# Selective attention followed by a SwiGLU block: attention output transposed on TensorE, bias rows copied on chip, q/k of the first head blocks on TensorE, loads re-ordered

**Chip, cores, metric.** One core of one Trainium2 chip. Times are device microseconds. Every run comes with a state, fast or slow, by its clock and its time.

## The reference, cut to what matters

```python
# q, k, v: (8 batches, 8 heads, 576, 64) f32;  s: (8, 8, 576)
scores = q @ k.T / 8 ; bias = -(cum[i] - cum[j]) with cum = cumsum(max(s, 0))
attn   = softmax(causal(scores + min(bias, 0))) @ v        # 64 heads
x      = attn, heads side by side                           # (4608 tokens, 512)
out    = (silu(x @ w_gate) * (x @ w_val)) @ w_out           # d_ff = 1536
```

The feed-forward part needs x with its 512 features on the partitions, so the attention output has to be transposed. A batch has 576 tokens, a feed-forward tile 512: tile t needs batches t-1 and t. There are nine tiles.

## The kernel before

One program order is written by hand: the heads of later batches are a generator of small items, and `pump` lays them between the matmuls of a tile. A head block is four heads. The parts that matter, with cuts marked `...`:

```python
raw bufs=2, otp bufs=2, wst bufs=2, xtp bufs=2      # SBUF buffers: raw q/k, output, raw weights, x

nc.scalar.dma_start(AUG, hl)                        # bias rows (high and low half, and negated) to DRAM
def aug(hb, eng):                                   # and from there into the k/q tiles: 4 loads a block
    ... eng.dma_start(T[...], AUG[hb * HB : ...])

def x_write(b): ...                                 # attention output of a batch to DRAM
def x_load(tt):                                     # and back, transposed by the DMA
    xts[tt] = xtp.tile([128, 4, TT], BF16, ...)
    nc.sync.dma_start_transpose(xts[tt], xdr[tt * TT : (tt + 1) * TT, :])

def side(hb, step):                                 # work for later blocks, laid beside head `step`
    ...
    if step == 0: aug(hb + 1, nc.sync); load_qk(hb + 2); cast k of hb + 1 (GpSimd)
    if step == 1: cast q of hb + 1; scratch(hb + 1)        # bf16 q/k to DRAM
    if step == 2: transposes(hb + 1)                       # and back, transposed by the DMA
    if step == 3: split(hb + 1, "k", ...); split(hb + 1, "q", ...)   # VectorE

def ffn_items(tt):
    for ft in range(12):
        pg = WG.T x (4 matmuls);  th = tanh (ScalarE);  pp = (th + 1) * pg (VectorE)
        pv = WV.T x (4 matmuls);  ht = pp * pv (VectorE)
    for ts_ in range(4):
        py = ht.T WO (12 matmuls);  copy (ScalarE);  store
```

Each engine works its own list in the order of the program, as the traces below show it (a mask on GpSimd comes only after eight copies, 4.10 us, that stand before it), and so does the queue of the SP engine, which issues nearly all loads.

Names in the profile lines: PE is TensorE, DVE VectorE, ACT ScalarE, POOL GpSimd, and a `q` behind a name is the engine's issuing of DMAs. `sc` are the scores, `pt` their exponentials (masked by GpSimd), `av` attention times V, `ot` its normalised value, `xps` the transposed `ot` in PSUM, the memory that TensorE writes, and `xt` the tile of x that `pg` and `pv` read; `xdr`, `augd`, `ks` and `qs` lie in DRAM, `pk` and `pq` are what comes back from the last two; `kq` holds k, q and the bias rows of a block, and `HL` all bias rows on chip; `wld` is a weight as loaded, `wg`, `wv` and `wo` are weights cast to bf16.

The softmax here doesn't subtract the row's maximum and nothing guards it: scores larger than these inputs give would overflow.

## Time and profile before

| | before |
|---|---|
| time | 490.84 us, median of 3 (487.07 to 491.25) |
| span of the profiled run | 486.5 us |
| busy share: TensorE / VectorE / ScalarE / GpSimd | 78 / 50 / 41 / 33 % |
| first `pg` matmul of the nine tiles | 75.4, 147.6, 196.3, 244.0, 292.0, 339.3, 382.1, 420.2, 451.3 us |

The starts come from the timeline: a tile begins with the first `pg` matmul after a `py`. Their differences (72, 49, 48, 48, 47, 43, 38, 31 us) are the best single summary: a tile is 144 matmuls of 0.216 us, 31.1 us, and whatever a tile takes above that is attention or waiting. The last two tiles have no heads left beside them.

### The profile page before, as it was taken

What the parts mean: (1) busy time and instruction counts of PE and PEld (TensorE: products, weight loads), DVE (VectorE), ACT (ScalarE), POOL (GpSimd) and SP (SyncE); (2) the same over time, 40 slices, a digit from 0 to 9 for tenths busy, and PEclk for the clock granted to TensorE, in tenths of its full rate; (3) what the DMA queues carried; (4) which work ended last, traced back from release to release, by engine and by line L of the source; (5) the groups of instructions that cost most, each with busy time, mean ns of one, the idle gap of its engine ahead of it and who ended that gap; (6) DMA issues with size and microseconds to landing.
All of it is one profiled execution on the core that took longest, in us unless ns stands there. A gap on an engine that the chain in (4) does not pass through costs nothing.

```text
span 486.5 us, 7669 instructions
## 1 busy us (share of the span) xinstructions
PE 379.5 (78%) x2844; PEld 205.6 (42%) x2896; DVE 241.8 (50%) x438; ACT 200.6 (41%) x406; POOL 159.5 (33%) x273
## 2 busy tenths in 40 slices
PE   0262325296958996899599959995999999999996
PEld 0251223153534553455345525552555554444442
DVE  3453340466615761576167616751775475273670
ACT  2152123044534553455346524652564663232321
POOL 8973133033531462236124612561255211000000
PEclk9997577588997999799889988998999999999999
DMA  9679887957598559845984698379743600701102
GB/s 177 153 211 202 246 221 154 271 140 223 144 214 195 116 131 233 202 106 140 246 189 97 160 232 198 79 186 229 180 77 110 168 2 5 203 13 45 43 0 88
DMA packets 118773, 73.33 MB, mean 151 GB/s; under 512 B 89424, under 2 KB 111440, under 8 KB 118736
## 3 DMA queue, kind: packets, MB, share of 16 engines
q1 hardware_dynamic: 117288, 68.19, 59.1%
q0 software_dynamic: 1264, 4.20, 2.8%
q8 instruction: 23, 0.38, 0.3%
q10 hardware_dynamic: 184, 0.46, 0.3%
q14 instruction: 14, 0.11, 0.1%
HBM read 38.19 MB, written 22.18 MB: 124 GB/s over the span
## 4 chain that ended last, share of the span: by engine, by line
PE 57%; DMA 16%; POOL 11%; SPq 5%; issue 5%; DVE 2%; ACT 1%; another core or an unknown queue 0%; POOLq 0%; ACTq 0%; DVEq 0%
PE pv L432 18%; PE pg L419 18%; PE py L443 11%; DMA xt<-xdr 7%; PE sc L264 6%; PE av L297 4%; SPq L120 3%; DMA wld<-in_moe_w_out_dram 3%; DMA rawq<-in_q_dram 3%; DMA wld<-in_moe_w_val_dram 2%; POOL cq L173 2%; POOL pt L276 1%; DMA wld<-in_moe_w_gate_dram 1%; DMA xdr<-ot 1%; POOL ck L173 1%
## 5 line engine op out<-in xcount | busy, mean ns | idle before, releaser
L272 ACT ACTIVATE pt<-sc 128x512 bf16<-128x512 f32 (+1 forms) x256 | 118.7, 503 | 88.8 <-PE sc L264 88.3
L419 PE MATMUL pg<-xt,wg 128*128 128x512 bf16 x412 | 115.7, 398 | 43.3 <-DMA xt<-xdr 30.7
L426 DVE SCALAR_TENSOR_TENSOR pp<-th,pg 128x512 bf16<-128x512 bf16 x108 | 74.0, 685 | 98.3 <-ACT th L424 97.4
L432 PE MATMUL pv<-xt,wv 128*128 128x512 bf16 x416 | 113.7, 392 | 4.6 <-DVE ht L437 3.5
L424 ACT ACTIVATE th<-pg 128x512 bf16<-128x512 f32 x108 | 64.5, 597 | 125.3 <-PE pg L419 118.9
L443 PE MATMUL py<-wo,ht 128*128 128x512 bf16 x416 | 103.0, 379 | 0.7
L276 POOL TENSOR_SCALAR_AFFINE_SELECT pt<-pt 128x512 bf16<-128x512 bf16 x64 | 41.6, 649 | 166.5 <-ACT pt L272 166.3
L264 PE MATMUL sc<-q,k 128*128 128x128 bf16 (+4 forms) x576 | 79.2, 255 | 18.2 <-DMA q<-augd 8.6
L437 DVE TENSOR_TENSOR ht<-pp,pv 128x512 bf16<-128x512 bf16 x108 | 74.1, 686 | 10.1 <-PE pv L432 1.2
L264 PEld LDWEIGHTS <-k 128*128 128x128 bf16 x576 | 49.6, 104 | 57.4 <-POOL q L138 8.8
L419 PEld LDWEIGHTS <-wg 128*128 128x128 bf16 x432 | 38.9, 101 | 78.7 <-issue 47.8
L297 PE MATMUL av<-vt,pt 128*128 128x65 bf16 x960 | 51.5, 198 | 22.1 <-DVE ot L313 20.4
L297 PEld LDWEIGHTS <-pt 128*128 128x128 bf16 x960 | 45.9, 101 | 49.7 <-issue 24.3
L432 PEld LDWEIGHTS <-wv 128*128 128x128 bf16 x432 | 38.3, 101 | 40.4 <-issue 8.6
L443 PEld LDWEIGHTS <-ht 128*128 128x128 bf16 x432 | 38.0, 98 | 35.3
L312 DVE RECIPROCAL rc<-av 128x5 f32<-128x5 f32 x64 | 12.2, 190 | 68.6 <-PE av L297 68.5
L451 ACT COPY ysb<-py 128x512 f32<-128x512 f32 x36 | 21.1, 586 | 51.8 <-PE py L443 45.7
L281 POOL TENSOR_SCALAR_AFFINE_SELECT pt<-pt 128x64 bf16<-128x64 bf16 x64 | 17.3, 271 | 69.6 <-ACT pt L272 68.9
L313 DVE TENSOR_TENSOR ot<-av,rc 128x320 bf16<-128x320 f32 x64 | 31.4, 491 | 2.2
L173 POOL CAST cq<-rawq 96x768 bf16<-96x768 f32 x30 | 23.9, 826 | 0.0
L173 POOL CAST ck<-rawk 96x768 bf16<-96x768 f32 x30 | 23.9, 825 | 0.0
L221 POOL CAST vt<-rawv 128x512 bf16<-128x512 f32 x32 | 18.7, 617 | 0.1
(48 smaller groups left out, 115.0 us busy)
## 6 DMA issues: line engine op xcount, KB each, us to landing
rawk<-in_k_dram SPq DMA_DIRECT2D x16, 576.0 KB
rawq<-in_q_dram SPq DMA_DIRECT2D x16, 576.0 KB
out_dram<-ysb SPq DMA_DIRECT2D x36, 256.0 KB
rawv<-in_v_dram SPq DMA_DIRECT2D x32, 256.0 KB
ks<-ck SPq DMA_DIRECT2D x14, 288.0 KB
qs<-cq SPq DMA_DIRECT2D x14, 288.0 KB
xdr<-ot POOLq DMA_DIRECT2D x7, 512.0 KB, 5.4
wld<-in_moe_w_gate_dram SPq DMA_DIRECT2D x4, 768.0 KB
```

What stands on the lines that cost most here:

```text
L173: eng.tensor_copy(cts[name, hb][:, r].rearrange("p j e d -> p e j d"), loaded[name, hb][:, 2 * r : 2 * r + 2, :, :],)
L264: nc.tensor.matmul(sc[:, o : o + w], kt[:, r * S + 128 * tj : r * S + 128 * (tj + 1)], qt[:, r * S + lo : r * S + hi], start=True, stop=True,)
L272: nc.scalar.activation(pt[:, CHUNK_PT[ci] : CHUNK_PT[ci] + o], sc[:, 0:o], AF.Exp, scale=0.125)
L276: nc.gpsimd.affine_select(pt[:, 1088:1600], pt[:, 1088:1600], pattern=[[0, 4], [1, 128]], compare_op=ALU.is_ge, fill=zreg, base=0, channel ...
L297: nc.tensor.matmul(av[:, bi * (D + 1) : (bi + 1) * (D + 1)], pt[:, c0 : c0 + 128], VT[b % 2][:, tj, h, :], start=(tj == 0), stop=(tj == bi),)
L313: nc.vector.tensor_mul(ot[:, :, h * D : (h + 1) * D], av3[:, :, 0:D], rc[:, :, None].to_broadcast([128, NCH, D]),)
L419: nc.tensor.matmul(pg, WG[j][:, c, f0 : f0 + 128], xt[:, c, :], start=(c == 0), stop=(c == 3),)
L424: nc.scalar.activation(th, pg, AF.Tanh, scale=0.5)
L426: nc.vector.scalar_tensor_tensor(pp, in0=th, scalar=1.0, in1=pg, op0=ALU.add, op1=ALU.mult)
L432: nc.tensor.matmul(pv, WV[j][:, c, f0 : f0 + 128], xt[:, c, :], start=(c == 0), stop=(c == 3),)
L437: nc.vector.tensor_mul(ht, pp, pv)
L443: nc.tensor.matmul(py, hts[ft][:, ts_ * 128 : (ts_ + 1) * 128], WO[ft // 3][:, ft % 3, :], start=(ft == 0), stop=(ft == NFT - 1),)
```

## The change

Its intent: no DRAM round trip for the attention output, none for the bias rows and for q/k of the first blocks, and loads in the order in which they are needed. The core of the diff (index details and renaming cut):

```diff
-raw bufs=2, otp bufs=2, wst bufs=2, xtp bufs=2
+raw bufs=3, otp bufs=3, wst bufs=3, xtp bufs=3

-    nc.scalar.dma_start(AUG, hl)
-                    eng.dma_start(T[...], AUG[hb * HB : ...])          # 4 per block, from DRAM
+                    eng.dma_start(KQ[hb % 2][e][a0 : a0 + 2, kq, ...], # 8 per block, SBUF to SBUF
+                                  HL[hb * HB + hh : hb * HB + hh + 1, :, :])
...
-        def x_write(b): ...
-        def x_load(tt): ...
+        def x_pe(pr):                       # a pair of heads, 576 tokens x 128 features
+            ps = mp.tile([128, S], BF16, tag="m", name="xps")
+            for c in range(NCH):            # 5 transposes
+                nc.tensor.transpose(ps[:, c * 128 : c * 128 + n], ot[0:n, c, :], ident[0:n, 0:n])
+            nc.vector.tensor_copy(xts[b + 1][:, r, 0 : S - n0], ps[:, n0:S])
+            nc.vector.tensor_copy(xts[b][:, r, TT - n0 : TT], ps[:, 0:n0])
...
         def side(h, step):
+            (h = 0: cast block 1 on VectorE, aug(1, nc.gpsimd), transpose it on TensorE)
+            (h = 1: load_qk(2); w_cast g0, v0, g1 and the next w_loads at steps 1 to 3)
-                    aug(hb + 1); load_qk(hb + 2); cast, scratch, transposes of block hb + 1
+            load_qk(h + 3); split and aug of block h + 1; cast, scratch, transposes of block h + 2
...
+                if not first and step == 0 and 2 <= h < 5:      # blocks 2, 3, 4
+                    aug(h, nc.sync)
+                    cast k, q on GpSimd; transpose on TensorE; copy by VectorE and ScalarE
...
-        LAG = 2.9
+        LAG = 1.65
+        hook = {1: w_cast v1, w_load g3;  2: load_v(1);  9: w_cast g2, w_load v3;
+                10: w_cast v2, w_load o0;  11: load_qk(3);  15: ...;  16: ...;  19: w_load o3;
+                21: load_qk(4);  22, 23: w_cast o2, o3}         # steps of tile 0
```

From block 5 on q/k still go through DRAM, but are cast and transposed two blocks ahead (h + 2), not one.

## The prediction

> **What bounds the kernel now.** The program first does attention for batch 0, then nine feed-forward tiles of 512 tokens, with the heads of later batches threaded between the matmuls. I read the slices first, then a table by stage (cut where a tile begins, at the first `pg` matmul after a gap), then the waits.
>
> ```profile
> PE   0262325296958996899599959995999999999996
> PEclk9997577588997999799889988998999999999999
> DMA  9679887957598559845984698379743600701102
> ```
> TensorE is idle most of the first quarter; from there it is full except for a dent every fourth slice, where the granted clock dips too. DMA is full in the first quarter.
>
> ```profile
> 0.00:24.00 24.00, 3.07 (x30) 2.45 (x31) 10.09 (x14) 4.67 (x7) 22.27 (x30) 1.00 0.84 167
> 24.00:75.00 51.00, 21.06 (x245) 16.45 (x245) 20.59 (x38) 15.83 (x38) 21.64 (x40) 0.75 0.84 212
> 75.00:96.00 21.00, 7.28 (x46) 3.44 (x45) 4.70 (x8) 4.56 (x11) 3.29 (x6) 0.66 0.89 228
> 96.00:147.60 51.60, 40.41 (x328) 22.60 (x335) 26.65 (x51) 21.91 (x46) 18.79 (x32) 0.90 0.75 185
> 147.60:196.30 48.70, 42.12 (x330) 22.77 (x336) 25.16 (x48) 23.37 (x48) 17.53 (x31) 0.92 0.72 166
> 339.20:382.00 42.80, 41.88 (x330) 22.67 (x336) 25.08 (x48) 22.95 (x48) 16.89 (x30) 0.96 0.58 135
> 417.20:450.00 32.80, 32.61 (x148) 14.72 (x151) 16.49 (x24) 10.01 (x17) 0.00 (x0) 1.00 0.32 81
> ```
> Columns: stretch and length, busy us of TensorE, its weight loads, VectorE, ScalarE, GpSimd, then granted clock, DMA share, GB/s. Two regimes. Up to 147.6 us only 71.8 us of TensorE work are done. After it (338.9 us) a tile with heads is 47 to 49 us long for some 42 us of TensorE work, and a tile without heads is 32.8. VectorE, ScalarE and GpSimd are busy 25, 23 and 18 us of those 48, so none is near being the bound.
>
> ```profile
> PE pg L419 <- DMA xt<-xdr: 30.7, 6, 6.9
> DVE wg L229 <- DMA wld<-in_moe_w_gate_dram: 29.2, 3, 13.9
> PE av L297 <- DVE ot L313: 20.4, 5, 14.5
> PE pg L419 <- DVE pp L426: 11.3, 1, 11.3
> PE sc L264 <- DMA q<-augd: 8.6, 1, 8.6
> PE sc L264 <- DVE q L195: 8.3, 1, 8.3
> ```
> Us in total, times, longest. The first line is the dent: each tile waits for its attention output to come back transposed from DRAM. The others lie before 97 us. VectorE, which works in order, sits on a weight cast whose load has not landed (13.9 us), and TensorE then seems to wait for VectorE (14.5 and 11.3 us); the real releaser is a DMA.
>
> ```profile
> 190.73 3.30 SPq L331 DMA_TRANSPOSE xt<-xdr  x1
> 196.34 1.87 PE L419 MATMUL pg<-xt,wg 128*128 128x512 bf16 x4 [6.26 <-DMA xt<-xdr]
> 202.28 1.03 PE L419 MATMUL pg<-xt,wg 128*128 128x512 bf16 x4
> ```
> Timeline, start and us. The transposing load is issued at 190.73 and lands 5.6 us later; four matmuls then take 1.87 us, not 1.03.
>
> **What the Trainium skill says.** "TensorE: Matmul & The Clock Gate", Part 1 (the HAM clock gate): after an idle window of about 3.4 us the array runs at half clock, and about 3.4 us of work brings it back. The trace agrees: a granted clock of 0.50 in the first 3 us after the gap at 147.6, 0.80 in the next 3. Each gap therefore costs about 1.5 + 0.6 = 2.1 us on top. The same page, Part 4 (PE-mode transpose): the result goes to PSUM and needs a copy; about 275 ns each in one kernel. Here a row of TensorE transposes shows 263 ns, but that is latency: four in a row end within 0.38 us. "DMA: Bandwidth & Descriptors", Issuing engines are not separate DMA queues: all issuers share the same 16 DMA engines, so the small bias copies sit among the big loads. The same page, Why small descriptors are slow: a fixed price per packet that hurts 256-byte packets. The trace's packets agree: stretches of 256-byte v packets ran near 200 GB/s, of weights (1,536 bytes) at up to 370, of q/k loads at about 240.
>
> **The change, part by part.**
>
> Removed: the DRAM round trip of the attention output (seven writes of 512 KB, eight of 64 KB, eight transposing loads); the DRAM bias table; the scratch write and transposing load of q/k for head blocks 2 to 4.
>
> Added on TensorE: five transposes per head pair instead of sixteen in the whole run. 576 columns at the pace of the 128x512 matmul (four back to back in 0.863 us, 0.42 ns a column) are 0.24 us, with starts about 0.35 us; 32 pairs, 11 us. q/k transposes for three more blocks: four groups of six, a group in 0.48 us where they run back to back, so 1.9 us a block, 5.8 us. On VectorE two copies per pair, about 0.6 us together by the 416 ns of the present 128x512 copy; a tile's 25 us becomes 28. ScalarE takes two 0.63 us copies for some blocks. None of this last lies on the path.
>
> Steady part, from tile 1 on. Before: 338.9 us. Waits for `xt` after 147.6: 30.7 - 6.9 = 23.8. Half clock after five gaps, tile 1's own included: 5 x 2.1 = 10.5. Added: 24 pairs x 0.35 = 8.4; block 4's q/k 1.9; block 4's bias rows, now fetched just before their scores, about 3; eight tile starts where the last transpose must be copied before `pg`, about 0.7 each (two copies and two handovers, less ten attention matmuls laid between) = 5.6. 338.9 - 34.3 + 18.9 = 323.5. Summed the other way (41 us for a tile with 8 heads without its gap, plus 1.4 and 0.7; five such tiles, the last with 6.4 heads; a first one of 47; two tiles of 33 and 34 without heads) it is 328. I take 325.
>
> Front part. First scores come at 23.2 us now, held by the bias rows, which went to DRAM and back. Copied on chip they land near 13, so scores start near 14. But GpSimd's order spoils this: memsets of the first k/q tiles (about 7.5 us by the 1.1 us rows), four bias copies at 0.6 to 0.8 us each (as its present DMA issues cost), the V tile's memsets 2.5, memsets of the second k/q tiles 7.2, five V casts 2.9, and then head 0's mask followed by eight more copies: its second mask comes at about 32. Heads 2 and 3 share VectorE with eight 0.75 us transpose copies (3.7 us each), later heads are ScalarE-bound (three exponentials of 596 ns and one of 224: 2.0, say 2.2 us), and two steps drain: tile 0 starts near 50 us, where now its first `pg` comes at 75.4 and it stalls until 96.
>
> Tile 0 is then limited by loads. Three weight buffers mean that the fourth weight is not asked for before the first cast, which stands in VectorE's order at head 5, near 43 us; the queue is empty by about 30. From 43 on the queue holds nine weight loads of 0.79 MB at 2.2 to 2.7 us (0.79 MB by 370 to 290 GB/s), two batches of v at 6, two blocks of q/k at 5 (1.18 MB each, by 200 and 240 GB/s) and two sets of bias copies at 2: 46 to 50 us, so until 89 to 93. The queue is in order and block 3's bias rows stand behind the last output weight, so head 12, due at step 20 of tile 0 (about 79 us: 50, 20 steps of 0.87 us, 0.7 us of attention in each from step 8 on, and 3 us of wait for block 2's bias rows), waits some 13 us. Sixteen steps remain, with 5.6 heads, some 23 us: tile 0 ends near 116, against 147.6 now. Saved: 31.
>
> Sum: 116 + 325 = 441 us of span. The run of 490.84 stands 4.3 above the profiled span of 486.5, so 445 measured; since the load positions look tuned to the step and I model the queue pessimistically, 442.
>
> **Rivals.** (1) The transposes are free and the front is bounded by TensorE: tile 0 from 46 to 95, total near 420. For: the 13 us wait in tile 0 is only an estimate. Against: DMA share is above 0.8 in the front already and every weight still has to pass there. (2) Loads spread worse than now: in-order VectorE stands at weight casts, as the 13.9 us wait shows it doing, and more q/k and v is asked for inside tile 0; it ends near 130, total 457. (3) The gaps come back in another form: PSUM has four rotating buffers for `pg`, `pv`, `py` and now for the transposes, and a handover TensorE, VectorE, TensorE at each pair may cost 1 us instead of 0.35: 24 x 0.65 = 16 more, 458. Against: VectorE has 20 us of slack a tile and the next attention matmuls stand between. (4) A busier array might be granted less clock; against it, 65 us of pure matmuls at the end run at 1.00.
>
> **Range and chances.** The steady part is known to about 6 us, the front to about 14; together 427 to 459 for 8 times in 10. All rivals stay over 5% below 490.84; only two of them together and a wait that I overlooked reach 480. Faster by over 2%: 0.97; within: 0.02; slower: 0.01.
>
> **What would show it.** Right: no wait on `xt` from a DMA; granted clock 1.00 from tile 1 on; tiles with heads 43 to 44 us apart, two near 33 at the end; tile 0 from about 50 to 116 with one wait of 10 us or more on bias rows or on a late weight cast; TensorE's first attention-times-V near 30 us, behind GpSimd. Wrong: waits on the copies of the transposed output of over 1 us per tile, tiles of over 46 us (the steady sum fails), tile 0 ending below 100 or above 128 (the queue model fails).

## The result

446.58 us, median of 4 (445.42 to 447.82), against 489.35 for the kernel before in the same rounds; ratio 0.9128, interval 0.9072 to 0.9184. Ratios here are the mean time of one kernel's fast runs over that of the other's of the same rounds, so not quite the ratio of the medians quoted. Predicted were 442, range 427 to 459: right, and by the right two parts, though not by each term.

The changed kernel's slices, same three rows as shown of before:

```profile
PE   0327859529899999999999999999999999999996
PEclk9998979858899999999999999999999999999999
DMA  9980688979579667945795598479161001001002
```

The dents are gone; TensorE is full and at full clock from the twelfth slice (from 123 us) on. What is left lies in front of it, where the DMA share is 0 in one slice (33 to 45 us), though loads are waited for soon after.

By stage, cut at the tile starts (50.9, 127.3, 169.3, 211.5, 253.9, 295.9, 338.1, 379.7 and 410.8 us), same columns as in the prediction:

```profile
0.00:14.00 14.00, 2.10 (x24) 1.86 (x24) 10.73 (x13) 1.13 (x1) 12.01 (x21) 1.00 0.98 184
14.00:50.90 36.90, 18.86 (x236) 14.24 (x238) 20.86 (x39) 16.36 (x37) 26.49 (x44) 0.95 0.68 180
50.90:64.60 13.70, 9.08 (x59) 4.57 (x59) 10.67 (x17) 5.53 (x9) 2.87 (x4) 0.92 0.77 176
64.60:98.20 33.60, 19.63 (x155) 11.26 (x159) 17.70 (x29) 12.99 (x26) 8.37 (x14) 0.75 0.91 224
98.20:127.30 29.10, 26.57 (x235) 15.67 (x241) 13.51 (x29) 15.81 (x33) 16.16 (x26) 0.85 0.75 177
211.50:253.90 42.40, 42.05 (x355) 23.59 (x359) 27.92 (x58) 23.53 (x49) 16.27 (x29) 1.00 0.73 165
379.70:410.80 31.10, 30.94 (x142) 14.07 (x144) 16.50 (x24) 9.51 (x16) 0.00 (x0) 1.00 0.09 35
```

A tile with heads is 42.4 us with 42.05 us of TensorE in it: next to nothing is left to gain from waits there. Of the 40.4 us between the two profiled spans (486.5 and 446.1), 20.3 come before tile 1 (147.6 to 127.3) and 20.1 after it (338.9 to 318.8).

The waits of the changed kernel (us in total, times, longest):

```profile
PE sc L260 <- DMA kq<-HL: 10.9, 3, 5.5
PE av L293 <- POOL pt L272: 6.7, 1, 6.7
PE sc L260 <- POOL kq L145: 2.8, 1, 2.8
```

No line of a `pg` waiting for a transposing load is left. And the timeline of the front, where the four things that the prediction says of it can be checked:

```profile
15.05 1.44 PE L260 MATMUL sc<-kq 128*128 128x128 bf16 x8 [2.84 <-POOL kq L145]
...
26.55 4.10 POOL L164 DMA_DIRECT2D kq<-HL  x8
26.65 0.84 PE L293 MATMUL av<-vt,pt 128*128 128x65 bf16 x12 [6.74 <-POOL pt L272]
...
30.96 0.35 PE L293 MATMUL av<-vt,pt 128*128 128x65 bf16 x3 [3.47 <-POOL pt L277]
...
41.98 0.95 DVE L242 CAST wg<-wld 128x1536 bf16<-128x1536 f32 x1
...
98.21 1.54 PE L260 MATMUL sc<-kq 128*128 128x128 bf16 x9 [5.53 <-DMA kq<-HL]
```

First scores at 15.05; attention-times-V held twice by GpSimd (the second time behind eight bias copies of 4.10 us together); the first weight cast, which lets the load queue go on, at 41.98; block 3's scores, held until 98.21. The releaser named in the first line is doubtful: that memset (13.95 us) fills the second pair of k/q tiles, which head 0 does not read. Head 0's bias rows had been moved by 13.0 us, by the trace's packets. What was still missing is q, copied out of PSUM by ScalarE from 14.16 on, behind its four bias copies and a table load of 1.28 us; in e10 below the same wait is put down to that copy.

### The profile page after: what moved, and what is told of

Same layout as the page of the kernel before. It is cut to its first block, busy times and chain, and to the rows that moved or that the text cites. A ratio compares the mean times of both kernels' runs of the same rounds, so it can differ in the third digit from the quotient of the medians.

```text
span 446.1 us, 8168 instructions
## 1 busy us (share of the span) xinstructions
PE 387.7 (87%) x3058; PEld 215.2 (48%) x3112; DVE 268.1 (60%) x501; ACT 207.7 (47%) x417; POOL 151.3 (34%) x262
## 4 chain that ended last, share of the span: by engine, by line
PE 76%; DMA 6%; POOL 5%; SPq 5%; DVE 4%; issue 2%; ACT 1%; ACTq 0%; POOLq 0%
PE pg L441 20%; PE py L465 19%; PE pv L454 19%; PE sc L260 9%; PE av L293 7%; SPq L125 4%; DMA wld<-in_moe_w_out_dram 3%; PE xps L325 2%; DMA kq<-HL 2%; DMA rawk<-in_k_dram 2%; DVE kq L217 1%; POOL vt L221 1%; POOL kq L164 1%; POOL ck L174 1%; POOL pt L272 1%
## 5 line engine op out<-in xcount | busy, mean ns | idle before, releaser
L454 PE MATMUL pv<-xt,wv 128*128 128x512 bf16 x411 | 110.7, 383 | 1.2 <-DMA kq<-HL 0.2
L441 PE MATMUL pg<-xt,wg 128*128 128x512 bf16 x416 | 110.4, 382 | 1.2 <-issue 0.4
L465 PE MATMUL py<-wo,ht 128*128 128x512 bf16 x415 | 104.6, 383 | 1.0 <-issue 0.2
L260 PE MATMUL sc<-kq 128*128 128x128 bf16 (+4 forms) x576 | 77.6, 252 | 16.2 <-DMA kq<-HL 10.9
L260 PEld LDWEIGHTS <-kq 128*128 128x128 bf16 x576 | 47.5, 103 | 50.7 <-issue 11.5
L293 PE MATMUL av<-vt,pt 128*128 128x65 bf16 x960 | 50.9, 198 | 13.9 <-POOL pt L272 6.7
L293 PEld LDWEIGHTS <-pt 128*128 128x128 bf16 x960 | 42.3, 100 | 33.1 <-POOL pt L272 7.0
L277 POOL TENSOR_SCALAR_AFFINE_SELECT pt<-pt 128x64 bf16<-128x64 bf16 x64 | 15.8, 247 | 63.7 <-ACT pt L268 63.7
L308 DVE RECIPROCAL rc<-av 128x5 f32<-128x5 f32 x64 | 12.2, 190 | 41.3 <-PE av L293 41.2
L221 POOL CAST vt<-rawv 128x512 bf16<-128x512 f32 (+1 forms) x40 | 27.4, 707 | 11.3 <-DMA rawv<-in_v_dram 11.2
L329 DVE COPY xt<-xps 128x64 bf16<-128x64 bf16 (+7 forms) x32 | 9.8, 305 | 32.5 <-PE xps L325 32.5
```

The costliest lines, as they stand in the source:

```text
L221: eng.tensor_copy(VT[b % 2][0:n, c, :, 0:D], loaded["v", b][0:n, c, :, :])
L260: nc.tensor.matmul(sc[:, o : o + w], T[:, 0, r * S + 128 * tj : r * S + 128 * (tj + 1)], T[:, 1, r * S + lo : r * S + hi], start=True, sto ...
L293: nc.tensor.matmul(av[:, bi * (D + 1) : (bi + 1) * (D + 1)], pt[:, c0 : c0 + 128], VT[b % 2][:, tj, h, :], start=(tj == 0), stop=(tj == bi),)
L441: nc.tensor.matmul(pg, WG[j][:, c, f0 : f0 + 128], xt[:, c, :], start=(c == 0), stop=(c == 3),)
L454: nc.tensor.matmul(pv, WV[j][:, c, f0 : f0 + 128], xt[:, c, :], start=(c == 0), stop=(c == 3),)
L465: nc.tensor.matmul(py, hts[ft][:, ts_ * 128 : (ts_ + 1) * 128], WO[ft // 3][:, ft % 3, :], start=(ft == 0), stop=(ft == NFT - 1),)
```

## The experiments

Two questions. First, which part of the change is the gain: the transposes on TensorE, or the order of loads and the lead of q/k? Second, is the front bounded as the prediction says, by GpSimd's order up to tile 0 and by the in-order load queue inside it? The theory of the prediction on the first: the waits on `xt` are the cost, remove them and they are gained. The rival: they hide other lateness.

The changed kernel's 446.58 us were measured in another session than the experiments. The kernel before ran in every session, with medians of 488.22 to 490.93 us, so a difference of 1 us from 446.58 says nothing, and one of 4 us or more is taken as real only where the trace moves with it.

### One part alone, and undone alone

**e5_before_x_pe**: the kernel before, with the output of every pair transposed on TensorE.

```diff
 # kernel before
-xtp bufs=2
+xtp bufs=3
-        def x_write(b): ...
-        def x_load(tt): ...
+        def x_pe(pr): ...          # as in the changed kernel, for all batches
```

> The kernel before with one part of the change alone: every head pair's attention output is transposed on TensorE, nothing goes to DRAM. Theory: the six waits on the transposing load (30.7 us) and the half clock after five of them (10.5 us) go, 28 more pairs cost about 0.3 us each (8 us): 453 to 460 us from 488, so that this part alone is worth some 32 of the 42 us of the whole change. Rival: the waits only hide other lateness (loads, masks), and at least half of them comes back: 470 us or more.

Measured 481.59 us, ratio 0.981 (0.9752 to 0.9867): 9 us instead of 32. The theory fell, the rival holds. By stage, three of its tiles:

```profile
143.00:192.60 49.60, 45.11 (x360) 24.53 (x358) 27.67 (x58) 23.40 (x49) 16.29 (x29) 0.93 0.66 150
192.60:237.10 44.50, 42.27 (x359) 23.47 (x357) 26.90 (x56) 23.42 (x48) 16.24 (x29) 1.00 0.67 157
327.00:374.10 47.10, 44.01 (x360) 24.16 (x358) 26.90 (x56) 23.48 (x48) 16.29 (x29) 0.96 0.57 125
```

And its waits (us in total, times, longest):

```profile
PE pg L405 <- DVE ht L423: 15.1, 10, 3.9
POOL pt L275 <- DMA rawk<-in_k_dram: 14.3, 3, 6.6
DVE k L194 <- DMA pk<-ks: 10.7, 5, 3.6
```

No wait on `xt` is left, yet the tiles are 44.5 to 49.6 us. TensorE now stands behind VectorE (`ht`), VectorE behind q/k that the DMA has not yet transposed (`pk`), GpSimd behind raw k; the list of the kernel before has none of these three waits. They have moved to the next thing that was late: with the gap in each tile, q/k one block ahead were just in time.

**e11_before_x_pe_ahead**: the same, plus the two-block lead from block 6 on (the kernel changes from one lead to the other beside block 4).

```diff
 # e5
-raw bufs=2
+raw bufs=3
 def side(hb, step):
     ...
-    aug(hb + 1); load_qk(hb + 2); cast, scratch, transposes, split of block hb + 1
+    if hb >= 5: load_qk(hb + 3); split, aug of block hb + 1; cast, scratch, transposes of block hb + 2
```

> The kernel before with the output transposed on TensorE (481.59 us) and, from block 6 on, q/k loaded, cast and transposed two blocks ahead, as the changed kernel does, instead of one. Theory (the gain of the removed gaps went into VectorE standing at late q/k, since a tile was then shorter than the one-block lead): tiles 3 to 5, 45 to 47 us there, come down to 42 to 43 and the time to 470 to 475 us. Rival (the rest is the price of the transposes themselves): 479 us or more.

Measured 467.16 us, ratio 0.955 (0.9512 to 0.9588). By tile:

```profile
187.00:229.30 42.30, 41.93 (x354) 23.48 (x359) 27.93 (x56) 23.45 (x49) 16.32 (x29) 1.00 0.73 167
313.70:355.90 42.20, 41.83 (x352) 23.38 (x357) 27.94 (x56) 23.42 (x48) 13.35 (x25) 1.00 0.35 79
```

42.2 us, the same as in the changed kernel, and the wait on `pk` shrank to 4.5 us; the time is a little below the range expected. So the steady part needs both edits: transposes on TensorE alone give 9 us, with the lead (and its third raw buffer) 22. The lead alone in the kernel before was not run. The tile in which the lead is built up (139 to 187 us) is still 47.8.

**e6_x_by_dram**: the changed kernel with the output of batches 1 to 7 written to DRAM and read back transposed.

```diff
 # changed kernel
+        def x_write(pr): two gpsimd.dma_start of ot to xdr, after each pair
         def x_pe(pr):
+            if b > 0:
+                if r == H // 2 - 1: nc.sync.dma_start_transpose(xts[b], xdr[b * TT : (b + 1) * TT, :])
+                return
```

> The changed kernel with that part undone alone: from batch 1 on the attention output is written to DRAM and read back by the transposing load before each tile; batch 0 stays on TensorE. Theory: seven gaps of 5 to 6 us with 2 us of half clock after each come back, less 0.3 us for each of 28 pairs: 446 + 40 to 50 = 480 to 495 us for gaps of the old size, at least 470. Rival (the gain lies in the front, through loads and bias rows): below 460 us.

Measured 504.11 us, ratio 1.0276 (1.0208 to 1.0344): slower than the kernel before. Its wait line:

```profile
PE pg L459 <- DMA xt<-xdr: 52.0, 7, 9.3
```

Seven gaps of 5.4 to 9.3 us, longer than the old ones of 5.3 to 6.9, and half clock after each. This part undone in the new order costs 57 us, done alone in the old order it gives 9: the parts do not add, and neither number is "the worth" of the transposes. The trace shows why the gaps are longer. Tile 2, first in the kernel before (its load and `pg` are in the prediction: 190.73 and 196.34 us), then in e6:

```profile
180.50 0.80 POOL L324 DMA_DIRECT2D xdr<-ot  x1
```

```profile
175.44 0.79 POOL L322 DMA_DIRECT2D xdr<-ot  x1
185.90 1.86 PE L459 MATMUL pg<-xt,wg 128*128 128x512 bf16 x4 [7.70 <-DMA xt<-xdr]
```

From the last write to `pg` it is 15.8 us before and 10.5 us in e6, which writes each pair by itself: the round trip is shorter. But TensorE runs out of work 9.6 us after that write before, and 2.8 us after it in e6; over all long gaps these are 7.8 to 9.6 and 1.0 to 2.8 us. The new order leaves less work behind the last head of a batch. That fits the smaller `LAG` (1.65 for 2.9), set for a path without a load; `LAG` alone was not changed in a run. So a part of the 57 us is the price of an order tuned to the path that e6 takes away.

**e7_transpose_twice**: each pair's five transposes and two copies done twice.

```diff
         def x_pe(pr):
+            for _again in range(2):
                 ps = mp.tile(...); 5 transposes; 2 copies
```

> The changed kernel doing the transposes and copies of each pair twice, to price them. If they cost TensorE's streaming time alone (0.24 to 0.35 us a pair, the second prediction term): 446 + 8 to 11 = 454 to 458 us. If each pair also costs a handover through the four PSUM buffers: 460 us or more. If they lie in holes: 448 us or less.

Measured 463.01 us, ratio 0.9421 (0.9374 to 0.9469). One tile of it:

```profile
216.70:261.50 44.80, 44.08 (x382) 24.80 (x379) 29.67 (x65) 23.49 (x48) 16.24 (x29) 1.00 0.69 157
```

44.8 against 42.2 us: 2.6 us for four more pairs, 0.65 us a pair. Ten transposes in a row take 0.91 us until the next instruction starts, so five cost 0.45 us. The run is above the 454 to 458 of my second term, in the range that I gave to a handover for each pair. The trace shows no such wait: TensorE is idle for 0.7 us in this tile, 0.35 in the changed kernel's. Of the 2.6 us the streams of four pairs are 1.8 and the longer idle time 0.4; the remaining 0.4 was not traced.

**e8_qk_all_pe**: q/k of all blocks transposed on TensorE.

```diff
-    NPE = 5
+    NPE = NHB
```

> All head blocks' q/k are transposed on TensorE, eleven blocks more than in the changed kernel, and no scratch goes to DRAM. The in-stream groups of six start 0.25 to 0.45 us apart, so 1 to 1.9 us a block: 11 to 21 us more TensorE time, plus waits of about 1 us a block on GpSimd's casts and on bias rows that are now asked for just before their scores: 460 to 480 us. Rival: with 13 MB less DMA traffic something else gets faster and it comes out even, 444 to 450 us.

Measured 475.56 us, ratio 0.9685 (0.9644 to 0.9727), as expected. A tile is 47.4 us instead of 42.2 for two blocks, 2.6 us a block. In this kernel the DMA's spare time is the cheaper place for q/k once a lead of two blocks hides it; five blocks on TensorE are a choice for the front only.

### The front

**e10_bias_dram**: bias rows through a DRAM table again.

```diff
+        nc.scalar.dma_start(AUGD, HL)
-                        HL[hb * HB + hh : hb * HB + hh + 1, :, :],
+                        AUGD[hb * HB + hh : hb * HB + hh + 1, :, :],
```

> The changed kernel with the bias rows written to DRAM once and read from there, all else kept. The first block's copies then wait for that write, some 3 to 5 us, and four of them are issued by GpSimd, which stands still meanwhile. Theory (GpSimd's order sets when attention goes on): TensorE's first attention-times-V starts 3 to 5 us later than 26.7 us, 449 to 452 us in all. Rival (only the first scores matter and these are hidden, or the steady part suffers from the detour): 445 to 448 us, or above 455 us.

Measured 446.82 us, ratio 0.9152 (0.9119 to 0.9186): the same as the changed kernel. The mechanism happened as the theory has it (first scores at 17.7 instead of 15.05, first attention-times-V at 29.9 instead of 26.65, tile 0 at 54.2 instead of 50.9 us), but the end did not move: tile 1 starts at 125.4 against 127.3. So the number fell in the rival's range while the start moved as the theory says: something inside tile 0 made up for it. What the SP engine needs to issue one bias copy, in the changed kernel and in e10 (ns, least, median, most):

```profile
L164 SPq DMA_DIRECT2D kq<-HL x112: 557/558/743, 61.8 to 336.2; - x112
L166 SPq DMA_DIRECT2D kq<-augd x112: 219/244/575, 65.0 to 332.1; - x112
```

Issuing a copy from SBUF holds the in-order queue more than twice as long as one from DRAM (558 for 244 ns). The first weight cast of e10 is 3.3 us late (45.24 for 41.98), but its queue catches up: block 3's scores are 1.1 us late (99.29), block 4's 0.2 us early. So e10 does not test a later start alone. Undone in the changed kernel, copying the bias rows on chip, one of the four parts in the change's title, gives nothing measurable: it gains 3.3 us up to tile 0 and loses them inside it.

**e4_bias1_act**: block 1's eight bias copies issued by ScalarE.

```diff
-                    aug(1, nc.gpsimd)
+                    aug(1, nc.scalar)
```

> The eight bias copies of block 1 are issued by ScalarE instead of GpSimd, where they took 4.1 us ahead of head 0's second mask. If GpSimd's order sets when attention can go on, TensorE's first full attention-times-V ends about 4 us earlier (27 us instead of 31), tile 0 starts near 47 instead of 50.9, and as the first weight cast and with it the load queue also come 4 us earlier, 442 to 444 us in all. If the load queue does not depend on it, or ScalarE's own exponentials are held up instead: 446 to 448 us.

Measured 441.87 us, ratio 0.9068 (0.9013 to 0.9123). Tile 0 starts at 46.0 and tile 1 at 121.1 us (from 50.9 and 127.3). Here the earlier start did carry through: VectorE's first weight cast, and so the restart of the load queue, came earlier with it (37.82 for 41.98 us), and the copies inside tile 0 are those of the changed kernel.

**e3_bias_early**: block 3's bias rows asked for with block 2's.

```diff
-                    aug(h, nc.sync)                      # at the first head of block h
+                    if h == 2: aug(2, nc.sync); aug(3, nc.sync)
+                    if h == 4: aug(4, nc.sync)
```

> Block 3's bias rows are asked for together with block 2's, ahead of the loads that they stood behind. If the 5.5 us wait of block 3's scores for its bias rows is the cost itself, it goes and 3 to 5 us are saved: 441 to 444 us. If it is only the last of a row of late loads (k of block 3 for GpSimd, the output weights for VectorE), the wait moves to these and at most 2 us are saved: 444.5 to 447 us. I expect the second.

Measured 445.56 us, ratio 0.9136 (0.9084 to 0.9189): as I expected, nothing that the interval shows. The 5.5 us wait is gone, but GpSimd waits longer for k (5.7 us instead of 4.0) and block 3's scores start at 95.6 instead of 98.2 us. The wait that a profile names last is not the price of that one load.

**e2_loads_late**: q/k of block 5 and v of batch 2 moved behind the last output weight.

```diff
-            if h >= 2 and h + 3 < NHB and step == 0:
+            if h >= 3 and h + 3 < NHB and step == 0:
                 load_qk(h + 3)
...                                                       # no load_v beside block 2
-            21: [lambda: load_qk(4)],
+            21: [lambda: load_v(2, range(5)), lambda: load_qk(4)],
-            23: [lambda: w_cast("o", 3)],
+            23: [lambda: w_cast("o", 3), lambda: load_qk(5)],
```

> Only the place of two loads in the queue is changed: q/k of block 5 and v of batch 2 (11 us of transfer by my sum) stand behind the last output weight instead of in front of it. Theory of the queue: the wait for block 3's bias rows, which ended at 98.2 us, ends near 89; some of it comes back because batch 2's v is cast on GpSimd in front of masks at heads 13 to 15; 438 to 443 us. If the queue is not the bound: 445 to 448 us.

Measured 449.46 us, ratio 0.9208 (0.9156 to 0.9259); both expectations missed. Block 3's scores did start at 89.0 us, as the queue theory says, but the moved loads were then late themselves. GpSimd and TensorE in its timeline:

```profile
109.32 1.59 POOL L174 CAST ck<-rawk 96x768 bf16<-96x768 f32 x2 [12.19 <-DMA rawk<-in_k_dram]
110.85 1.17 POOL L221 CAST vt<-rawv 128x512 bf16<-128x512 f32 x2
111.98 0.23 POOL L277 TENSOR_SCALAR_AFFINE_SELECT pt<-pt 128x64 bf16<-128x64 bf16 x1
...
112.27 0.34 PE L293 MATMUL av<-vt,pt 128*128 128x65 bf16 x3 [10.05 <-POOL pt L277]
```

GpSimd stands 12.2 us at the cast of block 5's k, the mask of the head at hand is behind it, and TensorE waits 10 us. What is put back in this queue is late in turn. The two runs of this section that gained by more than the noise, e4 and e1, are those that start the queue earlier.

**e1_casts_early**: the first weights cast while VectorE has nothing to do near 24 us, and the following loads asked for then.

```diff
 h = 0, step 1:
+                    w_cast g0, w_load v1;  w_cast v0, w_load g2;  w_cast g1, w_load v2
 h = 1, steps 1 to 3:
-                    (these)
+                    w_cast v1, w_load g3;  w_cast g2, w_load v3, load_v(1);  w_cast v2, w_load o0
 hook = {
-    1: w_cast v1, w_load g3;  2: load_v(1);  9: w_cast g2, w_load v3;  10: w_cast v2, w_load o0; ...
+    9: w_cast g3, w_load o1;  10: w_cast v3, w_load o2;  15: w_cast o0, w_load o3;  20: w_cast o1 ...
```

> The changed kernel took 446.58 us; this one casts the first weights in VectorE's idle time near 24 us instead of at head 5, and asks for the following weights and batch 1's v then, so that the load queue has no empty stretch between about 26 and 43 us. Theory (the front is bounded by the in-order load queue, which starts again only after the first cast): block 3's bias rows land near 84 us instead of 98, tile 0 ends near 113 us instead of 127.3, 430 to 436 us in all. Rival (tile 0 is bounded by TensorE, VectorE and their handovers; the late loads are only where the wait shows): tile 0 ends within 3 us of 127, 444 to 448 us.

Measured 439.16 us, ratio 0.9011 (0.8939 to 0.9082), between the two ranges expected. Block 3's scores start at 88.7 instead of 98.2, tile 1 at 117.2 instead of 127.3 us, although tile 0 starts later (53.2 for 50.9). So the late restart of the queue is a cause of the stall in tile 0, worth some 7 to 10 us of it; what bounds the rest was not tested. The edit also takes three weight casts (0.95 us each) out of VectorE's list in tile 0, and what that gives by itself is open.

### A faster version

**e9_best**: e1, e3 and e4 together, block 2's bias rows and q/k of block 3 asked for before tile 0.

```diff
 # e1, and:
-                    aug(1, nc.gpsimd)
+                    aug(1, nc.scalar)
                     load_qk(2)
+                    load_qk(3)                         # was at step 11 of tile 0
                     w_cast("v", 2); w_load("o", 0)
+                    aug(2, nc.sync)
-                    aug(h, nc.sync)
+                    if h == 2: aug(3, nc.sync)
+                    if h == 4: aug(4, nc.sync)
```

> The three edits that gained (early weight casts, bias rows of blocks 2 and 3 asked for early, block 1's bias copies issued by ScalarE) in one kernel, and q/k of block 3 asked for before tile 0. If the gains of 7.4, 1 and 4.7 us add, and the earlier q/k takes away the wait for GpSimd's casts near 83 us: 428 to 434 us. If they are the same wait met in three places: 437 us or more.

Measured 432.12 us, ratio 0.8865 (0.8821 to 0.8909): the three gains sum to 13.1 us, the run gained 14.5, with the earlier q/k of block 3 in it (and e3's 1 us was within the noise). They are not the same wait met three times. Tile 0 takes 62.9 us (48.8 to 111.7) instead of 76.3, and no gap of TensorE in it is over 1.8 us.

**e12_best_memset_dve**: the memsets of the second k/q tiles moved from GpSimd to VectorE.

```diff
-        init_kq(1, nc.gpsimd)
+        init_kq(1, nc.vector)
```

> The kernel of the last combination (432.12 us) with the memsets of the second k/q tiles, 7.5 us of GpSimd ahead of batch 0's V casts, done by VectorE, which waits there for block 1's k from 14.5 to 18.7 us. If GpSimd's order still sets when attention goes on, the first attention-times-V starts 5 to 7 us earlier than 28.7 us, tile 0 near 44 instead of 48.8, 426 to 429 us in all. If head 0's V casts are then bounded by v's landing, or block 1's q/k by VectorE: 430 us or more.

Measured 432.31 us, ratio 0.8801 (0.8754 to 0.8849); against e9 neither the medians nor the overlapping intervals show a difference. GpSimd was free earlier (head 0's mask at 17.5 instead of 27.4 us), but ScalarE in its timeline was not:

```profile
17.86 6.46 ACTq L164 DMA_DIRECT2D kq<-HL  x7
24.37 2.47 ACT L268 ACTIVATE pt<-sc 128x512 bf16<-128x512 f32 x6 [6.51 <-DVE wg L242]
```

ScalarE issues block 1's bias copies, which write into the tiles of those memsets, and its exponentials stand behind them for 6.5 us. (The line names a VectorE cast as releaser; by the first row it is the queue of copies.) In e9 ScalarE already stood there for 6.8 us, until 24.68, beside the wait on GpSimd. So two waits ran side by side, and taking away GpSimd's left ScalarE's.

## Why the prediction was right, step by step

- **Gaps and clock in the steady part.** The waits of 23.8 us and the half clock after them went, and the granted clock is 1.00 from tile 1 on, as said. 323.5 to 328 us, taken as 325, became 318.8.
- **Its terms.** "24 pairs x 0.35 = 8.4" was too small: 0.45 us a pair in TensorE's stream, 0.65 by e7, so 10.8 to 15.6. "eight tile starts ... 5.6" was too large: the attention matmuls laid between the last transpose and `pg` cover the copies, and all waits of `pg` sum to 1.2 us. "block 4's q/k 1.9" and its bias rows "about 3" fell into tile 0, not tile 1. With these put right the sum gives 315 to 320, around the 318.8 measured; the errors cancel in part.
- **What the sum left out.** It counts the removed waits as gained. e5 shows that this holds only together with the two-block lead, which the prediction did not mention at all: without it 9 us, with it 22. The prediction was right here because the change contains the lead, not because the step was argued. It even named the rival "the gaps come back in another form", but looked for that in PSUM and not in q/k.
- **Up to tile 0.** Scores near 14 (15.05), second mask near 32 (30.65), first cast near 43 (41.98), tile 0 near 50 (50.94). Working down each engine's list with the durations of before gave all four within 1.4 us; only the reason for the first is another: the bias rows were there near 13, as predicted, and the scores waited for ScalarE's copy of q.
- **Tile 0.** Block 3's bias rows were to land by 89 to 93; the scores started at 98.2. The predicted wait of 13 us is there in size: 4.0, 1.2, 2.9 and 5.5 us, 13.6 in all. But it is in four places (k and q for GpSimd, a copy by ScalarE, the bias rows), none over 10 us as its own list of signs asked, and e3 shows that the last alone is not the cost. The step "the queue is in order and block 3's bias rows stand behind the last output weight" is true and is not the bound by itself; the late restart of the queue is part of it, by e1. One term of the queue was plainly too small: "two sets of bias copies at 2". The two sets held the queue for 5.30 and 5.69 us (from 61.79 and from 93.73): 7 us more than assumed, which is in size the lateness of block 3's rows; no run shortened these copies alone.
- **The end of tile 0**, "sixteen steps ... some 23 us", took 29.1: block 4's transposes and bias rows are in it, and the granted clock of that stretch was 0.85, which I had not counted after a wait. With the 5 to 9 us of the line above this makes up the 11 us by which tile 0 ended later than "near 116". At 127.3 it ended 0.7 us short of the 128 that the prediction itself named as a failure of its queue model.
- **The sum**: 116 + 325 = 441 of span, measured 127.3 + 318.8 = 446.1. Front 11 us too short, steady part 6 us too long. The step from span to measured time was off as well: 4.3 us were added, from two different executions, where the changed kernel's profiled execution has 1.7 (447.82 for 446.1), and 3 us were taken off for a queue modelled "pessimistically", which was modelled too kindly. That the number came within 5 us is in part such cancelling.
- **Packets.** The prediction takes 370 GB/s for weights and 240 for q/k as agreeing with a price per packet. By the packets of its own trace q/k come in 1,536 bytes too, as the weights do, and ran at 229 to 261 GB/s (34 to 37 us, weights at 347 to 401 from 29 to 33); the packet's size does not explain that difference.

Left open: what bounds tile 0 once the queue restarts early; how much of e6's loss is `LAG`; and whether bias rows fetched from DRAM only inside tile 0 would keep the 3.3 us of the front and save the queue's time.

## What to carry to other kernels

A wait removed is gained only if everything else that the engine needs is early enough for the shorter loop; before counting it, look at how far ahead each other load and cast runs, and lengthen that lead in the same edit. Where engines and queues work their lists in order, find when each list restarts (here a weight cast at 41.98 us that stood at 22.87 in e1) rather than shortening the wait that shows up last. Parts of a change tested alone and undone alone can differ greatly (9 and 57 us here), so test both before saying what a part is worth, and look whether the order around it was tuned to it.

## What the Trainium skill lacked or had wrong

- "TensorE: Matmul & The Clock Gate", Part 4 (PE-mode transpose), gives about 275 ns for a transpose. A single one here shows 219 ns (median), but that is latency: ten in a row took 0.91 us until the next instruction, 91 ns each. The page has no figure for transposes in a row; taken as a price, its 275 ns would make the 160 transposes 44 us instead of some 15.
- The same section says that the full clock does not engage for transposes. Here 350 TensorE instructions a tile, 20 of them transposes, ran at a granted clock of 1.00 throughout; no run shows transposes alone for long, so this is not refuted.
- "DMA: Bandwidth & Descriptors", Issuing engines are not separate DMA queues, calls the time to initiate a DMA "usually small relative to the DMA itself". For one copy of 2.3 KB this holds: GpSimd took 0.52 us to issue it (median), and it landed 5.2 us after. But eight in a row held GpSimd for 4.10 us ahead of a mask, and issuing them elsewhere gave 4.7 us (e4).
- No page says that the source changes the time of an issue: SP took 558 ns (median) for a bias copy from SBUF and 244 ns for the same copy from DRAM (e10).
